# A two-layer decode step: the MLP's units in ten blocks of 128 and one of 96, in place of four padded stretches

## The chip, the cores and the metric

The kernel runs on one core of a Trainium2 chip. The metric is the device time of one execution in microseconds, as a median of several runs. All values are 32-bit floats.

## What is computed

One token `x` of 512 values goes twice through an attention block with a cached k and v, and a dense MLP. Both layers use the same weights and the same caches.

```python
def _A_ref(x, k_cache, v_cache, wq, wo):      # 32 heads, 4096 positions, 128 per head
    q = (x @ wq) by head
    scores = jnp.einsum("bhqd,bhkd->bhqk", q, k_cache) * (Dh ** -0.5)
    p = _softmax(scores, axis=-1)
    o = jnp.einsum("bhqk,bhkd->bhqd", p, v_cache)
    return o by token @ wo
def _B_ref(x, w1, b1, w2, b2):                # 512 -> 1376 -> 512
    h = _gelu(x @ w1 + b1)
    return h @ w2 + b2
x = x + _A_ref(_layernorm(x), k_cache, v_cache, wq, wo)
x = x + _B_ref(_layernorm(x), w1, b1, w2, b2)
x = x + _A_ref(_layernorm(x), k_cache, v_cache, wq, wo)
x = x + _B_ref(_layernorm(x), w1, b1, w2, b2)
```

The caches are 67 MB each and are read in both layers; w1 and w2 have 2.8 MB each.

## The kernel before, in words

The 32 heads are taken in eight groups of four. For each group, 8 MB of k and 8 MB of v come in loads over all 128 partitions into one large tile, `arena`, whose regions are used in turn. `scores` (L214) multiplies the query by k, `softmax` (L217 to L235) turns the scores into weights, `values` (L242) multiplies them by v, and `head_out` (L270, and L274 for the last group) multiplies by wo. Layer 0 goes through the groups upwards, layer 1 downwards, so that some of the caches stay in the arena from one layer to the next.

Every load goes through `load` (L84): the sync engine (SP) issues it to one hardware queue, in program order, when the region that it writes is free. The framework also lets SP hold a load until an earlier one has landed. TensorE's, VectorE's and SP's order near the MLP is written out by hand, by `pin`. `idle` (L374) is a matmul whose result nobody reads; some stand in the MLP between its steps.

`mlp` (L282) runs once in each layer. The 1376 hidden units are split into four stretches of 344, one for each quadrant `j` of 32 PSUM partitions, and the host pads each stretch of w2 and b1 with zeros to 352 = 11 x 32. `FB` = 11 counts the blocks of 32 units a quadrant, so a block is 128 units over all partitions. `HIDDEN` (L48) puts the blocks in three groups: 0 to 3, 4 to 7 and 8 to 10. `hidden(i)` (L290, matmuls at L296) computes one group with w1, 16 matmuls, each with the same number of columns: 128, 128 and 88. `turned` and `gelu` transpose the result and apply the activation, and L350 multiplies a block of 128 units by its 128 rows of w2, four matmuls a block (one for each quarter of the 512 outputs), adding up in `pM` over the eleven blocks. A 32-bit matmul stands as two instructions in the trace.

w1 is loaded once, in layer 0 (L476 and L487), and kept. w2 is loaded in each layer, in three parts over 128 partitions, `W2_PARTS` (L47): blocks 0 to 3, 4 to 7, 8 to 10 in layer 0, and 0 to 5, 6 to 8, 9 to 10 in layer 1. In layer 0 the last part takes the place of blocks 0 to 2, so it is issued in the middle of the MLP, behind block 3's matmuls (`follow`, L517 to L521, carried out at L352); behind it stand a piece of the next layer's k, and, behind the matmuls of blocks 5 and 7, two pieces of wq. In layer 1 the w2 parts are the last loads of the kernel (L477); behind them stands only the store of the output (L535).

Of the kernel before, what the change touches and what calls it, by code (L numbers as in the profile page):

```python
# [17 lines left out]
P = 128  # L18
D = 512
H, S, DH = 32, 4096, 128  # L20
F = 1376
G = 8
J = 4
C = 8
FJ = F // J
FB = 11
EPS = 1e-5
U = 512
KEPT = 6

NC = 4 * U
# [3 lines left out]
SPARE = 2 * BLOCK + STAY  # L35
# [4 lines left out]
AHEAD = 64  # L40
X_AT, B1_AT, B2_AT = 0, 8, 8 + FB
K2_HOME = 12 * NC

V1_HOME = *(2 * BLOCK + NC * c for c in range(5)), 8 * NC, 6 * NC, 7 * NC
W2_AT = tuple(SPARE + U * (c % 8) for c in range(FB)), tuple(2 * BLOCK + 2 * NC + U * c for c in range(FB))
PITCH = 1024
W2_PARTS = ((0, 4), (4, 8), (8, FB)), ((0, 6), (6, 9), (9, FB))  # L47
HIDDEN = ((0, 4), (4, 8), (8, FB))  # L48
W1_AT = (0, 4 * J * 32 * 4, 4 * J * 32 * 8)
# [10 lines left out]
def decode_layers(ctx: ExitStack, tc: tile.TileContext, k, v, w, w1, w2, out):  # L60
    nc = tc.nc
# [20 lines left out]
    arena = const.tile([P, ARENA], F32, name="arena")  # L82

    def load(at, src):  # L84
        t = arena[:, at : at + src.shape[-1]]
        tc.keep_in_program_order(nc.sync.dma_start(t, src))
        return t

    def pin(ins):
        tc.keep_in_program_order(ins)  # L90
# [34 lines left out]

    fixed = small("fixed", 2 * FB + 7)
    b1c, colsum, b2c = fixed[:, :FB], fixed[:, FB : 2 * FB], fixed[:, 2 * FB : 2 * FB + 4]
    negmean, one, power = (fixed[:, 2 * FB + 4 + i : 2 * FB + 5 + i] for i in range(3))
# [19 lines left out]
    pM, pN = pO[:, 2 * P : 3 * P], pO[:, 3 * P :]  # L148
# [7 lines left out]
    def of_32(t, n, i=0):  # L156
        return t[:, : 32 * n].rearrange("p (c q) -> p c q", q=32)[:, :, i]
# [15 lines left out]
    def mean_of(xs, s, at):  # L173
        nm = minus_mean(s, at)
        xc, sq, ss = small("xc", 4), small("sq", 4), small("ss")
        nc.vector.tensor_scalar(xc, xs[:, :, 0], nm, None, op0=ALU.add)
        nc.vector.scalar_tensor_tensor(sq, xc, 1.0, xc, op0=ALU.mult, op1=ALU.mult, accum_out=ss)
        return nm, ss, xc

    def rstd_of(ss, at):  # L180
        nv = minus_mean(ss, at)
        ve, r = small("ve"), small("rstd")
        tc.keep_in_program_order(
            nc.vector.tensor_scalar(ve, nv, -1.0, EPS, op0=ALU.mult, op1=ALU.add))
        nc.gpsimd.tensor_tensor(r, ve, power, op=ALU.pow)
# [96 lines left out]
    def mlp(xs, s, w1_t, w2_t, xb, rows, fill, follow):  # L282
        nm, ss, _ = mean_of(xs, s, pN[:, 0:1])
        nm_s, hs = small("nm_s"), pH[layer]
        if fill is None:
            nmr, cb, late = small("negm"), colsum, HIDDEN[0][1]
        nc.gpsimd.tensor_tensor(xb, xs[:, :, 0], b2c, op=ALU.add)
        nc.vector.tensor_copy(nm_s, nm)

        def hidden(i):  # L290
            at, first = hs[i], W1_AT[i]
            n = min(32 * HIDDEN[i][1], FJ) - 32 * HIDDEN[i][0]
            for c in range(4):
                for j in range(J):
                    f = first + n * (J * c + j)
                    pin(nc.tensor.matmul(at[32 * j : 32 * j + 2, :n], xs[:, c, :], w1_t[:, f : f + n],  # L296
                                         start=(c == 0), stop=(c == 3)))
                if i == 0 and c == VAR_AT:
                    rstd.append(rstd_of(ss, pN[:, 1:2]))
                    if fill is None:  # L300
                        nc.gpsimd.tensor_tensor(nmr, nm_s, rstd[0], op=ALU.mult)
                        nc.gpsimd.tensor_scalar(cb[:, late:], colsum[:, late:], nmr, None, op0=ALU.mult)
                        nc.gpsimd.tensor_tensor(cb[:, late:], cb[:, late:], b1c[:, late:], op=ALU.add)

        def turned(i):
            ht = work.tile([P, 32 * 4], F32, name="pt")
            n = HIDDEN[i][1] - HIDDEN[i][0]
            pin(nc.vector.transpose(ht[:, : 32 * n], hs[i][:, : 32 * n]))  # L308
            return ht

        def gelu(i, ht):
            b0, b1_ = HIDDEN[i]
            n = b1_ - b0
            h, u, g = (small("gelu_" + k, FB)[:, b0:b1_] for k in "hug")
            if fill is None and i > 0:
                pin(nc.vector.scalar_tensor_tensor(u, of_32(ht, n), rstd[0], cb[:, b0:b1_], op0=ALU.mult, op1=ALU.add))
            else:
                if i > 0:
                    nc.gpsimd.tensor_copy(colsum[:, b0:b1_], of_32(ht, n, 1))
                pin(nc.vector.scalar_tensor_tensor(h, of_32(ht, n, 1), nm_s, of_32(ht, n), op0=ALU.mult, op1=ALU.add))  # L320
                pin(nc.vector.scalar_tensor_tensor(u, h, rstd[0], b1c[:, b0:b1_], op0=ALU.mult, op1=ALU.add))
            nc.scalar.activation(g, u, AF.Gelu_apprx_tanh)
            if fill is not None and b1_ == FB:
                nc.scalar.activation(small("m"), g[:, :1], AF.Exp, scale=0.0)
            return g, turned(i + 1) if b1_ < FB else None

        rstd = []
        hidden(0)
        if fill is None:
            hidden(1)  # L330
            pin(nc.vector.transpose(rows[:, P : 2 * P], rows[:, :P]))
        ht = turned(0)
        if fill is not None:
            for _ in range(WARM):
                idle(fill, pO, 2 * P)
        hidden(1 if fill is not None else 2)
        if fill is not None:
            for _ in range(WARM):
                idle(fill, pO, 2 * P)
        for i, (b0, b1_) in enumerate(HIDDEN):  # L340
            if i == 1 and fill is not None:
                idle(fill, pS, 2 * P)
                hidden(2)
            g, ht = gelu(i, ht)
            if i == 1 and fill is not None:
                for _ in range(FILL):
                    idle(fill, pS, 2 * P)
            for c in range(b0, b1_):
                for j in range(J):
                    pin(nc.tensor.matmul(pM[32 * j : 32 * j + 1, :], g[:, c - b0 : c - b0 + 1],  # L350
                                         w2_t[c][:, P * j : P * (j + 1)], start=(c == 0), stop=(c == FB - 1)))
                for at, src in follow.get(c, ()):  # L352
                    load(at, src)
            if i == 1 and fill is not None:
                for _ in range(FILL - 1):
                    idle(fill, pS, 2 * P)
# [15 lines left out]
    w2_t = [[arena[:, at : at + U] for at in homes] for homes in W2_AT]  # L372
# [4 lines left out]
    for layer in range(2):  # L377
# [22 lines left out]
        for n, g in enumerate(order):  # L400
            first, final = n == 0, n == G - 1
# [65 lines left out]
            if layer == 1 and n == 0:  # L467
                wo_t = chunk(arena[:, PAIR : PAIR + NC])
            elif final:
                at = PAIR + NC * layer  # L470
                for a, b in WO_PARTS[layer]:
                    load(at + U * a, of_w(wo_at(g), 1)[:, U * a : U * b])
                wo_t = chunk(arena[:, at : at + NC])
                if layer == 0:
                    for i in range(2):
                        load(HELD + W1_AT[i], w1[:, W1_AT[i] : W1_AT[i + 1]])  # L476
                for a, b in W2_PARTS[layer][: 1 if layer == 0 else 3]:  # L477
                    load(W2_AT[layer][a], w2[:, U * a : U * b])
            else:
                t = load(PAIR, of_w(wo_at(g) if layer == 0 else wq_at(g - 1), 2))  # L480
                wo_t, wq_next = (chunk(t, i) for i in ((0, 1) if layer == 0 else (1, 0)))
            on = scaled_out_last(rl, pt, last_v, others) if final else scaled_out(rl, ot)
            if final:
                if layer == 0:
                    row_to_quadrants(row)
                    a, b = W2_PARTS[0][1]
                    load(HELD + W1_AT[2], w1[:, W1_AT[2] :])  # L487
                    load(W2_AT[0][a], w2[:, U * a : U * b])
                idle(last_v, pO, 256)
            head_out(on, wo_t, n)  # L490
            if final:
# [12 lines left out]
        at = work.tile([P, P], F32, name="pt")  # L504
# [7 lines left out]
            xb = of_32(ends, 4)  # L512
        follow = {}
        if layer == 0:
            a, b = W2_PARTS[0][2]
            first_k, next_wq = part(k, G - 2, 0, 1), of_w(wq_at(G - 2), 1)
            follow = {  # L517
                3: ((W2_AT[0][a], w2[:, U * a : U * b]), (SPARE + NC - U, first_k[:, NC - U :])),
                5: ((SPARE + NC, next_wq[:, : 2 * U]),),
                7: ((SPARE + NC + 2 * U, next_wq[:, 2 * U :]),),  # L520
            }  # L521
        mlp(x1, s1, w1_t, w2_t[layer], xb, *((None, last_v) if layer == 0 else (ends, None)), follow)
        if layer == 0:
# [4 lines left out]
            g = G - 2  # L528
# [9 lines left out]
def columns(a):  # L538

    return np.ascontiguousarray(a.reshape(J, 4, 32, -1).transpose(0, 2, 1, 3).reshape(P, 4, -1))  # L540
# [41 lines left out]
```

## Time and profile before

| | us |
|---|---|
| median of 3 runs | 677.32 (676.45 to 677.62) |
| the profiled execution | 677.48 |
| its span, first to last instruction | 675.6 |
| TensorE busy | 406.2 (60%) |
| VectorE busy | 115.1 (17%) |
| ScalarE busy | 27.3 (4%) |
| loads | 284.92 MB, 422 GB/s over the span |
| TensorE's mean granted clock | 0.798 |

The profiled execution is one run, and its span leaves out what lies ahead of the first instruction and behind the last. The trace names lines by the kernel's source, and a line can be that of a helper: all loads stand at L86. `in_w` stands for the three weight tensors alike. "DMA share" is the mean busy share of the sixteen DMA engines.

### The profile page before, as it was taken

What the parts mean: (1) busy time and instruction counts of PE and PEld (TensorE: products, weight loads), DVE (VectorE), ACT (ScalarE), POOL (GpSimd) and SP (SyncE); (2) the same over time, 40 slices, a digit from 0 to 9 for tenths busy, and PEclk for the clock granted to TensorE, in tenths of its full rate; (3) what the DMA queues carried; (4) which work ended last, traced back from release to release, by engine and by line L of the source; (5) the groups of instructions that cost most, each with busy time, mean ns of one, the idle gap of its engine ahead of it and who ended that gap; (6) DMA issues with size and microseconds to landing.
All of it is one profiled execution on the core that took longest, in us unless ns stands there. A gap on an engine that the chain in (4) does not pass through costs nothing.

```text
span 675.6 us, 6748 instructions
## 1 busy us (share of the span) xinstructions
PE 406.2 (60%) x3012; PEld 110.6 (16%) x3012; DVE 115.1 (17%) x369; ACT 27.3 (4%) x57; POOL 5.0 (1%) x24
## 2 busy tenths in 40 slices
PE   2644664465534854466798987574466544744797
PEld 1111111111111110111125321111111111110124
DVE  3002111121021201211022322120121011200212
ACT  0000000000000000001011200000000000000010
POOL 1000000000000000000000000000000000000000
PEclk9758767797678866877799998976797677975989
DMA  9999999999999999999999999999999999999996
GB/s 374 435 436 435 436 435 435 414 456 432 423 432 417 449 435 436 431 435 414 434 406 354 418 423 438 425 434 436 433 437 435 429 435 409 453 436 411 432 413 249
DMA packets 11268, 285.34 MB, mean 422 GB/s; under 512 B 1252, under 2 KB 1256, under 8 KB 3688
## 3 DMA queue, kind: packets, MB, share of 16 engines
q1 hardware_dynamic: 11240, 284.92, 98.6%
q8 instruction: 23, 0.38, 0.2%
q14 instruction: 5, 0.04, 0.0%
HBM read 284.92 MB, written 0.00 MB: 422 GB/s over the span
## 4 chain that ended last, share of the span: by engine, by line
PE 40%; DMA 39%; another core or an unknown queue 15%; DVE 4%; ACT 1%; issue 1%; ACTq 0%; SPq 0%; DVEq 0%
DMA arena<-in_v 34%; PE pO L242 20%; PE pS L214 12%; DMA arena<-in_w 4%; PE pB L270 4%; PE pO L208 1%; ACT arena L224 1%; PE pS L375 1%; PE pO L226 1%; DVE arena L246 1%; DVE smalls L218 1%; PE pO L375 0%; PE pO L350 0%; DVE arena L206 0%
## 5 line engine op out<-in xcount | busy, mean ns | idle before, releaser
L214 PE MATMUL pS<-arena,smalls 128*8 128x512 f32 x1024 | 145.9, 722 | 110.9 <-DMA arena<-in_k 110.1
L242 PE MATMUL pO<-arena,pt 128*4 128x512 f32 x1008 | 142.8, 714 | 84.3 <-DMA arena<-in_v 83.8
L214 PEld LDWEIGHTS pS<-arena,smalls 128*8 128x8 f32 x1024 | 30.0, 102 | 211.2 <-issue 190.5
L270 PE MATMUL pB<-arena,smalls 128*1 128x512 f32 x112 | 52.0, 608 | 20.0 <-DVE smalls L251 15.9
L242 PEld LDWEIGHTS pO<-arena,pt 128*4 128x4 f32 x1008 | 28.8, 97 | 186.5 <-issue 183.7
L218 DVE TENSOR_REDUCE smalls<-pS 128x1 f32<-128x512 f32 x16 | 11.1, 692 | 249.2 <-PE pS L214 249.2
L246 DVE STREAM_TRANSPOSE arena<-pO 128x512 f32<-128x512 f32 x16 | 11.5, 717 | 225.7 <-PE pO L242 225.7
L226 PE MATMUL pO<-ident,arena 128*128 128x128 f32 x64 | 13.2, 341 | 37.9 <-ACT arena L224 37.6
L224 ACT ACTIVATE arena<-pS,smalls 128x512 f32<-128x512 f32 x16 | 12.4, 777 | 535.7 <-DVE smalls L223 535.7
L206 DVE SCALAR_TENSOR_TENSOR arena<-arena,smalls 128x512 f32<-128x512 f32 x45 | 33.8, 752 | 1.6
L270 PEld LDWEIGHTS pB<-arena,smalls 128*1 128x1 f32 x112 | 8.5, 85 | 63.0 <-issue 35.2
L208 PE MATMUL pO<-smalls,arena 128*128 128x1 f32 x120 | 16.6, 260 | 3.3 <-DVE arena L206 3.3
L208 PEld LDWEIGHTS pO<-smalls,arena 128*128 128x128 f32 x120 | 15.3, 200 | 15.8 <-DVE arena L206 13.8
L226 PEld LDWEIGHTS pO<-ident,arena 128*128 128x128 f32 x64 | 8.5, 169 | 51.9 <-ACT arena L224 46.4
L375 PE MATMUL pO<-arena,ident 128*8 128x256 f32 (+1 forms) x42 | 14.4, 470 | 0.0
L375 PE MATMUL pS<-arena,ident 128*8 128x512 f32 (+1 forms) x34 | 14.0, 517 | 0.5 <-DVE pt L308 0.5
L204 DVE TENSOR_SCALAR arena<-arena,smalls 128x512 f32<-128x512 f32 x15 | 7.2, 481 | 2.7 <-DMA arena<-in_w 2.7
L209 DVE COPY smalls<-pO 128x4 f32<-128x4 f32 x15 | 2.5, 165 | 25.7 <-PE pO L208 25.7
L170 PE MATMUL pO<-smalls 128*32 128x1 f32 x64 | 2.0, 184 | 7.4 <-DVE smalls L164 6.4
L350 PE MATMUL pO<-arena,smalls 128*1 128x128 f32 x176 | 6.0, 272 | 0.7 <-DMA arena<-in_w 0.7
L230 DVE STREAM_TRANSPOSE smalls<-smalls 128x32 f32<-128x32 f32 x16 | 3.4, 212 | 17.4 <-ACT arena L224 17.4
L375 PEld LDWEIGHTS pO<-arena,ident 128*8 128x8 f32 x42 | 3.8, 90 | 7.9 <-issue 6.3
(92 smaller groups left out, 102.6 us busy)
## 6 DMA issues: line engine op xcount, KB each, us to landing
arena<-in_k SPq DMA_DIRECT2D x8, 4096.0 KB, 26.9
arena<-in_w SPq DMA_DIRECT2D x13, 2048.0 KB, 33.3
arena<-in_v SPq DMA_DIRECT2D x2, 4096.0 KB, 38.0
arena<-in_k SPq DMA_DIRECT2D x3, 2048.0 KB, 14.2
arena<-in_v SPq DMA_DIRECT2D x2, 2048.0 KB, 41.2
arena<-in_w SPq DMA_DIRECT2D x4, 1024.0 KB, 16.3
arena<-in_w SPq DMA_DIRECT2D x6, 512.0 KB, 12.1
arena<-in_v SPq DMA_DIRECT2D x2, 1024.0 KB, 42.9
```

Source lines behind the costliest of these rows:

```text
L204: pin(nc.vector.tensor_scalar(t, wt[:, 0, :], xc[:, 0:1], None, op0=ALU.mult))
L206: nc.vector.scalar_tensor_tensor(t, wt[:, c, :], xc[:, c : c + 1], t, op0=ALU.mult, op1=ALU.add)
L208: nc.tensor.matmul(at[:, j : j + 1], t[:, P * j : P * (j + 1)], one, start=True, stop=True)
L214: nc.tensor.matmul(pS[32 * j : 32 * j + C, :], z[:, j, C - 1 - c : 2 * C - 1 - c], kt[:, j, :], start=(c == 0), stop=(c == C - 1))
L218: nc.vector.tensor_reduce(mx[:, 0:1], pS, axis=AX.X, op=ALU.max)
L224: nc.scalar.activation(p, pS, AF.Exp, bias=bias[:, 0:1], scale=sc, accum_out=mx[:, 0:1])
L226: nc.tensor.transpose(pT[:, b].rearrange("p j r -> p (j r)"), p[:, P * b : P * (b + 1)], ident)
L242: nc.tensor.matmul(pO[32 * j : 32 * j + 4, :], pt[:, j, c, :], by_head(vt)[:, j], start=(i == 0), stop=(i == of - 1))
L246: nc.vector.transpose(ot[:, :512], pO)
L270: nc.tensor.matmul(pB[0:1, :], on[:, d : d + 1], wt[:, d, :], start=n == 0 and d == 0, stop=n == G - 2 and d == 3)
L350: pin(nc.tensor.matmul(pM[32 * j : 32 * j + 1, :], g[:, c - b0 : c - b0 + 1], w2_t[c][:, P * j : P * (j + 1)], start=(c == 0), stop=(c == ...
L375: pin(nc.tensor.matmul(at[:C, :n], ident[:, :C], t[:, 0, :n], start=True, stop=True))
```

## The change

The units are split without stretches: block `c` has units 128c to 128c + 127, and quadrant `j` has 32 of them; block 10 has only 96, so its fourth quadrant has none. w1 is laid out anew by the host with the same number of bytes, `hidden` gives each quadrant its own number of columns (in the third group 96, 96, 96 and 64), and w2 is padded at its end alone. `load_w2` loads the parts of w2. A part that holds block 10 comes as two loads: one over partitions 0 to 95 with all of its blocks, and one over partitions 96 to 127 with all but block 10. Block 10's matmuls read 96 rows. In layer 0 the last part is still issued behind block 3, ahead of the piece of k.

```diff
+FULL = F - P * (FB - 1)
...
+    def load_w2(layer, a, b):
+        at, whole = W2_AT[layer][a], min(b, FB - 1)
+        if b < FB:
+            load(at, w2[:, U * a : U * b])
+            return
+        pin(nc.sync.dma_start(arena[:FULL, at : at + U * (b - a)], w2[:FULL, U * a : U * b]))
+        if whole > a:
+            pin(nc.sync.dma_start(arena[FULL:, at : at + U * (whole - a)], w2[FULL:, U * a : U * whole]))
...
         def hidden(i):
             at, first = hs[i], W1_AT[i]
-            n = min(32 * HIDDEN[i][1], FJ) - 32 * HIDDEN[i][0]
+            b0, b1_ = HIDDEN[i]
+            ns = [32 * (b1_ - b0 - (b1_ == FB and j == J - 1)) for j in range(J)]
             for c in range(4):
-                for j in range(J):
-                    f = first + n * (J * c + j)
+                for j, n in enumerate(ns):
+                    f = first + sum(ns) * c + sum(ns[:j])
...
             for c in range(b0, b1_):
                 for j in range(J):
-                    pin(nc.tensor.matmul(pM[32 * j : 32 * j + 1, :], g[:, c - b0 : c - b0 + 1],
-                                         w2_t[c][:, P * j : P * (j + 1)], start=(c == 0), stop=(c == FB - 1)))
-                for at, src in follow.get(c, ()):
+                    rows_ = FULL if c == FB - 1 else P
+                    pin(nc.tensor.matmul(pM[32 * j : 32 * j + 1, :], g[:rows_, c - b0 : c - b0 + 1],
+                                         w2_t[c][:rows_, P * j : P * (j + 1)], start=(c == 0), stop=(c == FB - 1)))
+                for at, src in follow.get(c, ()) if c else ():
                     load(at, src)
+                if layer == 0 and c == 3:
+                    load_w2(0, *W2_PARTS[0][-1])
+                    for at, src in follow[0]:
+                        load(at, src)
...
                 for a, b in W2_PARTS[layer][: 1 if layer == 0 else 3]:
-                    load(W2_AT[layer][a], w2[:, U * a : U * b])
+                    load_w2(layer, a, b)
...
-            a, b = W2_PARTS[0][2]
             first_k, next_wq = part(k, G - 2, 0, 1), of_w(wq_at(G - 2), 1)
             follow = {
-                3: ((W2_AT[0][a], w2[:, U * a : U * b]), (SPARE + NC - U, first_k[:, NC - U :])),
+                0: ((SPARE + NC - U, first_k[:, NC - U :]),),
...
-    pad = 32 * FB - FJ
-    w2 = np.pad(a["w2"].reshape(J, FJ, D), ((0, 0), (0, pad), (0, 0)))
-    b1 = np.pad(a["b1"].reshape(J, FJ), ((0, 0), (0, pad)))
+    w2 = np.pad(a["w2"], ((0, P * FB - F), (0, 0))).reshape(FB, P, D)
+    b1 = np.pad(a["b1"], (0, P * FB - F)).reshape(FB, P)
...
```

## Rows read from the trace of the kernel before

**Rows 1.** The page: the span in 40 slices, and the hardware queue's packets, MB, share.

```profile
GB/s 374 435 436 435 436 435 435 414 456 432 423 432 417 449 435 436 431 435 414 434 406 354 418 423 438 425 434 436 433 437 435 429 435 409 453 436 411 432 413 249
...
q1 hardware_dynamic: 11240, 284.92, 98.6%
```

**Rows 2.** Busy time by stretch: length, engines (instructions), granted clock, DMA share, GB/s.

```profile
30.00:610.00 580.00, 346.26 (x2440) 91.91 (x2432) 97.41 (x305) 24.37 (x50) 1.78 (x6) 0.79 1.00 428
```

**Rows 3.** The chain of waits in the tail: start us, us, what.

```profile
627.56 32.33 DMA arena<-in_v
...
659.90 12.08 DMA arena<-in_w
...
672.02 0.66 PE pO L350 x16
...
672.71 0.29 DVE arena L534
```

**Rows 4.** The timeline in the tail, w2's matmuls: start, us, instructions, [idle before <-releaser].

```profile
668.95 1.49 PE L350 MATMUL pO<-arena,smalls 128*1 128x128 f32 x48
...
670.77 0.84 PE L350 MATMUL pO<-arena,smalls 128*1 128x128 f32 x24 [0.32 <-DMA arena<-in_w]
...
672.02 0.62 PE L350 MATMUL pO<-arena,smalls 128*1 128x128 f32 x16 [0.42 <-DMA arena<-in_w]
```

**Rows 5.** Busy time by stretch in the tail.

```profile
666.00:667.00 1.00, 0.79 (x33) 0.49 (x37) 0.49 (x6) 0.00 (x0) 0.20 (x1) 1.00 1.02 408
...
669.00:670.00 1.00, 1.00 (x47) 0.96 (x44) 0.73 (x3) 0.21 (x1) 0.08 (x1) 1.00 0.29 119
```

**Rows 6.** SP's own timeline at the turn, 364 to 371 us.

```profile
364.21 0.33 SPq L86 DMA_DIRECT2D arena<-in_w  x1
364.63 0.38 SPq L86 DMA_DIRECT2D arena<-in_k  x1
368.10 0.80 SPq L86 DMA_DIRECT2D arena<-in_w  x2
370.21 0.33 SPq L86 DMA_DIRECT2D arena<-in_k  x1
```

**Rows 7.** Loads issued from 352 to 380 us: count, size, us to landing.

```profile
arena<-in_w SPq DMA_DIRECT2D x2, 512.0 KB, 4.2
...
arena<-in_w SPq DMA_DIRECT2D x1, 768.0 KB, 5.0
...
arena<-in_k SPq DMA_DIRECT2D x1, 256.0 KB
```

**Rows 8.** The timeline at the turn: w1's matmuls, and w2's for the last blocks.

```profile
360.71 1.05 PE L296 MATMUL pS<-arena,smalls 128*2 128x128 f32 x32
...
364.83 0.79 PE L296 MATMUL pS<-arena,smalls 128*2 128x88 f32 x32
...
369.29 0.57 PEld L350 LDWEIGHTS pO<-arena,smalls 128*1 128x1 f32 x24 [0.47 <-issue]
369.32 0.83 PE L350 MATMUL pO<-arena,smalls 128*1 128x128 f32 x24
```

**Rows 9.** Busy time by stretch at the turn, quarters of a microsecond.

```profile
364.50:364.75 0.25, 0.25 (x2) 0.00 (x0) 0.00 (x0) 0.00 (x0) 0.00 (x0) 1.00 0.55 229
...
368.50:368.75 0.25, 0.25 (x3) 0.12 (x2) 0.00 (x0) 0.00 (x0) 0.00 (x0) 1.00 0.32 123
...
369.50:369.75 0.25, 0.25 (x16) 0.24 (x12) 0.00 (x0) 0.00 (x0) 0.00 (x0) 1.00 0.16 66
369.75:370.00 0.25, 0.25 (x17) 0.22 (x6) 0.00 (x0) 0.00 (x0) 0.00 (x0) 1.00 0.81 279
```

**Rows 10.** What SP waited for at the turn, 340 to 380 us: total, times, longest.

```profile
SPq L86 <- PE pO L350: 3.1, 3, 1.3
```

**Rows 11.** SP's own timeline at 628 us.

```profile
628.42 0.80 SPq L86 DMA_DIRECT2D arena<-in_v  x2
```

**Rows 12.** Loads issued from 620 us on: count, size, us to landing.

```profile
arena<-in_v SPq DMA_DIRECT2D x2, 512.0 KB, 33.6
```

More of the change, by code (lines that the diff above doesn't have):

```diff
@@ L487, in decode_layers @@
                     load(HELD + W1_AT[2], w1[:, W1_AT[2] :])
-                    load(W2_AT[0][a], w2[:, U * a : U * b])
+                    load_w2(0, a, b)
                 idle(last_v, pO, 256)
@@ L545 @@
         x=A_x, k=A_k_cache, v=A_v_cache, wq=A_wq, wo=A_wo, w1=B_w1, b1=B_b1, w2=B_w2, b2=B_b2).items()}
-    pad = 32 * FB - FJ
-    w2 = np.pad(a["w2"].reshape(J, FJ, D), ((0, 0), (0, pad), (0, 0)))
-    b1 = np.pad(a["b1"].reshape(J, FJ), ((0, 0), (0, pad)))
-    w1 = columns(a["w1"]).reshape(P, 4, J, FJ)
+    w2 = np.pad(a["w2"], ((0, P * FB - F), (0, 0))).reshape(FB, P, D)
+    b1 = np.pad(a["b1"], (0, P * FB - F)).reshape(FB, P)
+    w1 = columns(a["w1"])
     wq = columns(a["wq"]).reshape(P, 4, G, J, J, 32)
@@ L557 @@
         (X_AT, columns(a["x"])[:, :, 0]),
-        (B1_AT, b1.reshape(J, FB, 32).transpose(0, 2, 1).reshape(P, FB)),
+        (B1_AT, b1.T),
         (B2_AT, columns(a["b2"])[:, :, 0]),
@@ L565 @@
         w=w,
-        w1=np.concatenate([w1[..., 32 * a : 32 * b].reshape(P, -1) for a, b in HIDDEN], axis=1),
-        w2=w2.reshape(J, FB, 32, D).transpose(0, 2, 1, 3).reshape(P, FB * D),
+        w1=np.concatenate([w1[:, c, f : f + 32] for a, b in HIDDEN for c in range(4) for j in range(J)
+                           for f in range(P * a + 32 * j, min(P * b, F), P)], axis=1),
+        w2=w2.transpose(1, 0, 2).reshape(P, FB * D),
     )
```

## The prediction

> **What bounds the kernel now.** I first read the page by slices and by queue [rows 1]. In 37 of the first 39 slices the DMA engines moved 406 GB/s or more, and the loads of the one hardware queue took 98.6% of what sixteen engines could give in the span. So the kernel is a stream of 284.92 MB, and TensorE, 60% busy, is not the bound. Over the long middle the granted clock is 0.79 and the stream still moves 428 GB/s [rows 2]. In the units of the profile's size column (1024 bytes) that is 418 KB a microsecond. Two places remain where the change touches anything that may set the end: the turn between the layers, near 364 us, and the tail after 660 us.
>
> In the tail the chain of waits [rows 3] goes from a load of v to a load of w and from there straight to the last sixteen w2 instructions, the last addition and the store. The timeline [rows 4] shows the same from the engine's side: the 48 instructions of blocks 0 to 5 run without a wait, block 6 waits for a load until 670.77, and block 9 waits for the last part of w2 until 672.02. So this end is loads, to the last byte, although the queue is no longer full: by the stretches of one microsecond [rows 5], 408 GB/s moved in the 667th microsecond, 119 in the 670th. Some of the sixteen engines have finished and the slowest still works. Its pace is what counts: 1.25 us for the last 512 KB (670.77 to 672.02), or 410 KB/us, nearly the pace of the full stream.
>
> At the turn the last part of w2 (768 KB) is issued at 364.21 [rows 6] and lands 5.0 us later [rows 7], at 369.21. The matmuls that read it begin at 369.32, and what stood before their first weight load is named "issue", not a DMA [rows 8]. So the part lands about 0.1 us ahead of its use. After it the queue runs dry: 123 and then 66 GB/s at 368.5 and 369.5 [rows 9], because the next issue, at 368.10, stood behind a w2 matmul [rows 6, 10].
>
> **The change part by part.** The sum is made against the profiled execution: 677.48 us, a span of 675.6 and 1.88 around it, 0.16 above the median of 677.32.
>
> *Bytes.* w1 keeps its size: 16 pieces of 344 columns become, for the last blocks, three of 96 and one of 64 for each of four input rows, 352 in all as four of 88 were. w2 sheds 32 rows of its last block: 32 x 2 KB = 64 KB in each layer. The turn's load falls from 768 KB to 576 + 128 = 704, the tail's from 512 to 384 + 64 = 448.
>
> *Tail.* At the slowest engine's 410 KB/us, 64 KB are 0.16 us; at the stream's 418 they are 0.15. If rows spread over all engines as now, each engine has an eighth less of that part, and the landing moves from 672.02 to 671.87. No row shows a load over 96 or 32 partitions: all before cover 128 (the output's four rows aside). So the price is bounded: -0.15 us from below. From above, I take the row in which about half of the engines were at work: share 0.55 and 229 GB/s, 224 KB/us [rows 9]. Were both narrow loads held to that, 448 KB would take 2.0 us in place of 1.25, or +0.75. I take -0.15, because the nearest rows, those of the laggard tail, show each engine emptying its own share without waiting for the others.
>
> *Turn.* 64 KB less is 0.15 us of the queue again, but the queue runs dry there until TensorE releases the next issue, so a shorter load only lengthens the gap: I take 0. The bounds: -0.15, should the slowest engine be the one that never runs dry (369.21 plus 0.6 us for the 256 KB behind it [rows 7] is 369.8, just where the next load's data begin), and at half rate 704 / 224 = 3.1 us in place of 768 / 418 = 1.8, or +1.3, of which 0.1 is slack before the matmuls.
>
> *The added issues.* SP puts out two loads where it put out one; the distance from one issue to the next is 0.42 us (364.21 to 364.63) [rows 6]. At the turn the first 256 KB of k stand behind it and leave 0.42 later. Their matmuls are in the next layer, and SP then idles from 365.0 to 368.10, so the issues behind that are not moved. Without that cover it would be 0.42 us. In the tail SP has nothing behind it but the store at 673. But the added load takes a wait: SP holds each late load until the one eight issues before has landed, as the chain shows where the last part leaves at 659.90 with the landing of a v load issued at 627.56 [rows 3]. The added one waits for the next v load, issued at 628.42, with a median of 33.6 us to landing [rows 11, 12], thus until about 662.0. The load ahead of it lands at 670.77, so 8.8 us cover it: 0.
>
> *Matmuls.* The third group of hidden units is 96 wide where it was 88. Its instructions took 0.79 us at 88 columns and 1.05 at 128 [rows 8], so 6.5 ns a column, 0.05 us for eight more (the fourth quadrant, with 64, runs beside the others). In the tail it ends before the wait that ends at 670.77, so 0. At the turn it stands on TensorE's path, moves the issue at 368.10 to 368.15 and the later k loads as much. They find the loads before them still moving (two of 512 KB [rows 7], 2.4 us of the stream from about 369.75 [rows 9]), so I take 0, at most +0.05. Eight w2 instructions have 96 rows in place of 128: sixteen took 0.62 us [rows 4], so eight 0.31, and half of that either way would be 0.16 in each layer; no row has 96, the nearest have 128 and the same columns, and I take 0. VectorE and ScalarE do the same work on the same shapes.
>
> Sum: 677.48 - 0.15 = 677.33, and with the 0.16 between profiled run and median, 677.2.
>
> [...] The tail's rows show that late engines finish alone [rows 5], which is why I count the saving at all. [...]
>
> **The rivals.**
> *Serial.* The 96-row load takes as long as the whole part did, and the 32-row load follows at half the stream's rate. Tail: 64 KB at 224 KB/us, +0.29. Turn: 128 KB, +0.57, less 0.1 of slack, then TensorE is late by 0.47 and with it the k loads that wait for it. It decides from the point where the two together end later than 369.32. Sum +0.76: 678.1. For it: the even split of 128 rows over sixteen engines is gone. Against it: the slowest engine works alone at the end and meets nobody. [...]
> *Half.* Both narrow loads run on half of the engines. Tail +0.75, turn +1.2: 679.3, slower. For it: nothing but the missing row; against it: loads of 128 rows keep all sixteen at work [rows 1], and the length of a row stays what it was in the first of the two.
> *All bytes count.* The slowest engine never runs dry at the turn: -0.30, 677.0. For it: 369.8 against 369.75 above. Against it: what follows at 370.21 waits for matmuls.
> *Lag relieved.* The new split takes rows off just the engine that ends last. At most it saves the whole 1.25 us of the last part, and 0.15 at the turn: 675.9. For it: only the drain in [rows 5].
>
> **How the numbers follow.** Forecast 0.60, serial 0.18, all bytes count 0.11, half 0.07, lag relieved 0.04. About 0.2%, 1.35 us, is what a measurement can tell from no change. Forecast and all bytes count are within it, serial too (+0.8) with a small share beyond; half is beyond it (+2.0), the lag's relief just so (-1.4). So faster 0.04, same 0.86, slower 0.10. The range goes from all bytes count less the spread of the three runs (0.87 below their median), 676.2, to serial plus 0.6 of the same spread, 678.7; half and the lag's relief are left out.
>
> **What would show it.** The queue's bytes should fall by 0.13 MB. In the tail the last w2 matmuls should start about 1.1 us after block 6's wait ends, not 1.25; 1.5 says serial, 2.0 half. At the turn the last w2 matmuls should follow their filler matmuls with no DMA as releaser; a DMA wait of half a microsecond says serial, one of over a microsecond half. An issue of the k loads moved by more than 0.1 us with no such wait, or a stream below 428 GB/s in the middle, would mean that I have missed what the change touches.

## The result, and the profile after

The change makes the kernel slower: 680.5 us (679.85 to 681.48, six runs) against 677.62 (six runs beside it), a ratio of 1.0043 with a 95% interval of 1.0032 to 1.0054, so 2.9 us (2.2 to 3.7). The profiled execution took 680.87 us, with a span of 678.8, 3.2 us more than before. The forecast was 677.2, with a range up to 678.7.

The bytes are what the prediction said, 0.13 MB fewer on the page's queue line [rows 1]:

```profile
q1 hardware_dynamic: 11272, 284.79, 98.5%
```

The middle of the stream is not slower. From 30 to 360 us both kernels moved 429 GB/s, and from 380 to 610 both moved 433. What changed stands at the two places where w2's last part is loaded.

**The turn.** The timelines of SP and of TensorE after, against [rows 6] and [rows 8]:

```profile
364.22 0.34 SPq L95 DMA_DIRECT2D arena<-in_w  x1
364.61 0.42 SPq L97 DMA_DIRECT2D arena<-in_w  x1
365.12 0.37 SPq L87 DMA_DIRECT2D arena<-in_k  x1
368.63 0.82 SPq L87 DMA_DIRECT2D arena<-in_w  x2
372.15 0.33 SPq L87 DMA_DIRECT2D arena<-in_k  x1
```

```profile
364.90 0.84 PE L307 MATMUL pS<-arena,smalls 128*2 128x96 f32 x32
...
367.95 1.05 PE L362 MATMUL pO<-arena,smalls 128*1 128x128 f32 x32 [0.27 <-DMA arena<-in_w]
...
371.26 0.84 PE L362 MATMUL pO<-arena,smalls 128*1 128x128 f32 x24 [1.41 <-DMA arena<-in_w]
```

The two narrow loads leave when the one did. But TensorE now waits for a load before the last blocks, which it starts at 371.26 in place of 369.32, and the load of k behind them leaves at 372.15 in place of 370.21: 1.94 us later, and so do the next k loads. The matmuls of blocks 4 to 7 also wait a little, at 367.95. The loads' own rows say why (issued from 352 to 380 us: size, us to landing; the first line is of before, the others of after, against [rows 7]):

```profile
arena<-in_w SPq DMA_DIRECT2D x1, 1024.0 KB, 12.7
```

```profile
arena<-in_w SPq DMA_DIRECT2D x1, 1024.0 KB, 13.2
...
arena<-in_w SPq DMA_DIRECT2D x1, 576.0 KB, 6.5
...
arena<-in_w SPq DMA_DIRECT2D x1, 128.0 KB, 6.5
```

The 576 KB land 6.5 us after their issue, though the 768 KB took 5.0, and the 1 MB ahead of them, whole in both kernels, lands 0.5 us later too. That is no scatter: issued at 354.3 to 354.9 us in every trace, this load took 13.2 to 14.4 us in the five kernels with the narrow loads or the halves behind it (after, and below e2, e6, e8, e10), and 12.6 to 12.9 in the six others, e7 and e11 among them. The stretches of one microsecond show what the DMA engines did meanwhile (the last three columns are the granted clock, the DMA share and GB/s):

```profile
365.00:366.00 1.00, 0.74 (x32) 0.49 (x27) 0.12 (x1) 0.00 (x0) 0.10 (x1) 1.00 0.95 217
...
367.00:368.00 1.00, 0.73 (x8) 0.17 (x9) 0.00 (x0) 1.00 (x1) 0.00 (x0) 1.00 0.98 248
368.00:369.00 1.00, 1.00 (x33) 0.86 (x34) 0.00 (x0) 0.43 (x2) 0.00 (x0) 1.00 1.02 201
369.00:370.00 1.00, 0.85 (x6) 0.18 (x2) 0.00 (x0) 0.00 (x0) 0.00 (x0) 1.00 1.09 184
```

This is the line to learn to read: a share near 1 and 200 GB/s. A dry queue shows a low share at a low rate, as in [rows 9] (0.16 at 66); here the engines are busy all the time, 0.98 to 1.09, and move 184 to 248 GB/s, about half of the 429 of the long middle. One such microsecond alone proves little: before has 0.83 at 168 GB/s from 369 to 370, as loads begin, and after has 0.89 at 182 from 373 to 374, when the narrow loads have landed. From 367 to 370, three in a row with 0.98 or more at 184 to 248, are what before does not have; the loads by themselves below show it for 19 us on end.

**The tail.** The chain of waits and w2's matmuls after, against [rows 3] and [rows 4]:

```profile
629.12 34.28 DMA arena<-in_v
...
663.41 11.67 DMA arena<-in_w
...
675.22 0.66 PE pO L362 x16
```

```profile
672.07 1.49 PE L362 MATMUL pO<-arena,smalls 128*1 128x128 f32 x48 [0.65 <-DMA arena<-in_w]
...
674.11 0.84 PE L362 MATMUL pO<-arena,smalls 128*1 128x128 f32 x24 [0.55 <-DMA arena<-in_w]
675.22 0.62 PE L362 MATMUL pO<-arena,smalls 128*1 128x128 f32 x16 [0.27 <-DMA arena<-in_w]
```

The last matmuls start 1.11 us after block 6's, where it was 1.25: the sign that the prediction had named for itself is there. It proves nothing, because the whole loads ahead are late: blocks 0 to 5 waited for no load before and do now. The first narrow load leaves at 662.14, just as the last part did at 659.90 when the third v load had landed, and the last matmuls start 13.08 us later, where they started 12.12 later. These lines do not tell how much of that is lost in the tail itself; e2 and e3 below do. The windows again have a high share at half the rate:

```profile
669.00:670.00 1.00, 0.90 (x40) 0.77 (x40) 0.56 (x5) 0.00 (x0) 0.19 (x1) 1.00 0.91 207
```

### The profile page after: what moved, and what is told of

Read it like the earlier page. It is cut to its first block, busy times and chain, and to the rows that moved or that the text cites. A ratio compares the mean times of both kernels' runs of the same rounds, so it can differ in the third digit from the quotient of the medians.

```text
span 678.8 us, 6751 instructions
## 1 busy us (share of the span) xinstructions
PE 405.4 (60%) x3012; PEld 110.3 (16%) x3012; DVE 115.4 (17%) x369; ACT 27.3 (4%) x57; POOL 5.0 (1%) x24
## 4 chain that ended last, share of the span: by engine, by line
DMA 48%; PE 34%; another core or an unknown queue 13%; DVE 3%; issue 1%; ACT 1%; SPq 0%; ACTq 0%
DMA arena<-in_v 34%; PE pO L252 17%; PE pS L224 9%; DMA arena<-in_w 7%; DMA arena<-in_k 6%; PE pB L280 4%; PE pO L218 1%; PE pO L236 1%; PE pO L391 1%; ACT arena L234 1%; DVE arena L256 1%; DVE smalls L228 1%; PE pO L362 0%; DVE arena L216 0%
## 5 line engine op out<-in xcount | busy, mean ns | idle before, releaser
L252 PE MATMUL pO<-arena,pt 128*4 128x512 f32 x1008 | 138.1, 701 | 81.2 <-DMA arena<-in_v 80.8
L391 PE MATMUL pO<-arena,ident 128*8 128x256 f32 (+1 forms) x42 | 14.4, 470 | 0.0
L362 PE MATMUL pO<-arena,smalls 128*1 128x128 f32 (+1 forms) x176 | 6.0, 272 | 3.1 <-DMA arena<-in_w 3.1
L307 PE MATMUL pS<-arena,smalls 128*2 128x128 f32 (+2 forms) x160 | 5.0, 259 | 0.3 <-DMA arena<-in_w 0.2
## 6 DMA issues: line engine op xcount, KB each, us to landing
arena<-in_k SPq DMA_DIRECT2D x3, 2048.0 KB, 14.4
```

The source lines that it names most:

```text
L252: nc.tensor.matmul(pO[32 * j : 32 * j + 4, :], pt[:, j, c, :], by_head(vt)[:, j], start=(i == 0), stop=(i == of - 1))
L362: pin(nc.tensor.matmul(pM[32 * j : 32 * j + 1, :], g[:rows_, c - b0 : c - b0 + 1], w2_t[c][:rows_, P * j : P * (j + 1)], start=(c == 0), s ...
L391: pin(nc.tensor.matmul(at[:C, :n], ident[:, :C], t[:, 0, :n], start=True, stop=True))
```

## The experiments

The theory after the comparison: a load of fewer than 128 rows is slow for the rows that it writes, with the engines held meanwhile, as in the share of 0.98 to 1.09 above. The rivals: the new layout and its matmuls; the second load, with its issue and its wait; the number of rows as such; the rows that it reads.

### Undone, and at one place alone

```diff
 def load_w2(layer, a, b):
-    if b < FB:
+    if True:                       # e1: whole in both layers
...
+    if b < FB or layer == 1:       # e2: narrow in layer 0 alone
...
+    if b < FB or layer == 0:       # e3: narrow in layer 1 alone
```

e1: 

> The changed kernel with w2's last part loaded whole again, over 128 rows (768 and 512 KB), in both layers; the new layout of the units stays. If the narrow loads are the cause: the time of before, 677.6 (677.2 to 678.0), and the last w2 matmuls of layer 0 again near 369.3 without a wait for a load. If the layout, the 96-column matmuls or the 96-row matmuls are the cause: it stays near 680.5.

e2: 

> The changed kernel with the narrow loads in layer 0 alone; layer 1's last part is whole. If the turn passes its delay on to the end: about 1.9 to 2.2 us over before, so 679.5 to 679.8. If the stream makes up for the turn's delay in layer 1 and the tail is what costs: 677.6 to 678.0.

e3: 

> The changed kernel with the narrow loads in layer 1 alone; layer 0's last part is whole. If the two places add up: about 1.0 us over before, 678.6, and the loads of w2 ahead of the narrow ones land later than before by most of that. If the tail costs nothing: 677.5.

| | us | ratio to before, 95% |
|---|---|---|
| e1, whole in both | 677.0 | 0.9997 (0.9988 to 1.0006) |
| e2, narrow in layer 0 | 678.85 | 1.0023 (1.0015 to 1.0032) |
| e3, narrow in layer 1 | 678.29 | 1.0019 (1.0009 to 1.0029) |

With whole loads the changed layout takes the time of before, so neither the layout nor the matmuls of 96 columns and 96 rows cost anything that can be measured. The turn costs 1.6 us (1.0 to 2.2), the tail 1.3 (0.6 to 2.0), and the two make up the 2.9. In the median the turn's price is below the 1.9 that I expected, which its interval still holds: of the 1.94 us by which k loads were late near 380 us, the load of v near 415 kept 1.63 (415.94 against 414.31) and the load of k near 564 kept 1.40. Later issues do not tell: the load of v near 582 left 3.10 us later, the first one near 625 only 0.70.

e2 also shows how not to read the tail. Its loads there are all whole, and yet the last matmuls start 13.00 us after the last part was issued, as in after and not as before (chain of waits):

```profile
660.27 12.96 DMA arena<-in_w
673.27 0.66 PE pO L362 x16
```

What separates the two is how much was left to move. From 640 to 660 us and from 660 to 680, before moved 412 and 185 GB/s, 11.94 MB in all, e2 417 and 214, 12.62 MB, and after 418 and 218, 12.72 MB. By an estimate at 430 GB/s, near the 429 and 433 of the long stretches, e2's 0.68 MB more than before are 1.6 us, and it starts its last matmuls 1.25 later; after's 0.78 MB are 1.8 us, and it starts them 3.20 later. So in after some 1.4 us are lost past 640 us, which agrees with the tail's 1.3.

In e3's trace the whole loads ahead of the narrow ones are the late ones. The loads issued from 620 us on, first e1 and then e3:

```profile
arena<-in_w SPq DMA_DIRECT2D x1, 1536.0 KB, 16.3
...
arena<-in_w SPq DMA_DIRECT2D x1, 768.0 KB, 13.2
```

```profile
arena<-in_w SPq DMA_DIRECT2D x1, 1536.0 KB, 18.2
...
arena<-in_w SPq DMA_DIRECT2D x1, 768.0 KB, 15.2
```

Both of e3's are 2 us later than e1's, though they are whole in both. (e3's profiled execution is longer than its median, so the 2 us are that run's.) Over all traces the 768 KB took 14.5 to 16.2 us in the five with the narrow loads or the halves behind them in the tail, 13.2 to 13.6 in five others and 14.2 in e2, where the stream alone was late. Why these loads are late is not shown.

### A second load, but of whole rows

```diff
-        pin(nc.sync.dma_start(arena[:FULL, at : at + U * (b - a)], w2[:FULL, U * a : U * b]))
-        if whole > a:
-            pin(nc.sync.dma_start(arena[FULL:, at : at + U * (whole - a)], w2[FULL:, U * a : U * whole]))
+        load(at, w2[:, U * a : U * whole])
+        load(at + U * (whole - a), w2[:, U * whole : U * b])
```

> The last part in two loads as in the change, but cut by blocks and not by rows: all blocks but the last over 128 rows, then block 10 over 128 rows; bytes as before. If a second load, its issue and its wait are the cost: near 680.5. If it is the number of rows: 677.6 (677.2 to 678.0).

676.75 us, 0.9994 (0.9985 to 1.0002). The second issue and its wait are covered, as the prediction had it.

### Loads by themselves

Eight loads in a row from SP into eight places, and a small write by VectorE to each place when it has landed; the next stage waits for all. Nothing else of the reference is computed, and each of these kernels (e5, e9, e12) ran once.

```python
for i, (a, b) in enumerate(stage):
    nc.sync.dma_start(places[i][a:b, :], k[s % G][a:b, N * i : N * (i + 1)])
for i in range(8):
    nc.vector.memset(places[i][:, :8], 0.0)
```

> Loads of k alone, nothing else of the reference: twelve stages of eight loads, each row 8 KB; a stage starts when the one before has landed. Rows by stage: 128; 0-95; 96-127; 0-95 and 96-127 in turn; 0-63; 64-127; 0-63 and 64-127 in turn; 0-111; 0-31; 128 and 0-95 in turn; 128 and 96-127 in turn; 128. Whole loads move about 430 GB/s: 8.4 MB in 19.5 us plus some 2 us of start. If a narrow load only has fewer bytes: 0-95 takes 14.6, 96-127 4.9, 0-63 9.8 plus the start. If it runs on half of the engines: double these (29, 9.8, 19.5), with a DMA share near 0.5. If all engines work but get in each other's way at the rows' side: a share near 1 at about half the rate, 0-95 in 19.5 or more, and the stages that mix narrow and whole loads slower than the sum of their parts at their own rates.

VectorE's writes give the landings (start, us, instruction, idle before). Two each from the stages of 0-95, 96-127 and 128 rows, all of 8 KB a row:

```profile
41.97 0.07 DVE L45 MEMSET place<- 128x8 f32 x1 [3.03 <-DMA place<-in_k]
45.05 0.07 DVE L45 MEMSET place<- 128x8 f32 x1 [3.01 <-DMA place<-in_k]
...
62.24 0.07 DVE L45 MEMSET place<- 128x8 f32 x1 [1.23 <-DMA place<-in_k]
63.52 0.07 DVE L45 MEMSET place<- 128x8 f32 x1 [1.22 <-DMA place<-in_k]
...
251.13 0.07 DVE L45 MEMSET place<- 128x8 f32 x1 [2.43 <-DMA place<-in_k]
253.62 0.07 DVE L45 MEMSET place<- 128x8 f32 x1 [2.43 <-DMA place<-in_k]
```

Read the distance from one start to the next: 2.49 us a load of 128 rows, 3.08 of 96, 1.28 of 32. The load of 96 rows takes longer than the one of 128, with a quarter less in it. By stages (length, VectorE, GpSimd, clock, DMA share, GB/s; in this order 0-95, 96-127, 128 rows):

```profile
34.00:53.00 19.00, 0.39 (x6) 0.00 (x0) 1.00 1.01 254
59.00:67.00 8.00, 0.39 (x6) 0.00 (x0) 1.00 0.84 166
248.00:262.00 14.00, 0.39 (x6) 0.00 (x0) 1.00 1.01 425
```

The share of 0-95 is 1.01: the engines are all held, so it isn't half of them at work. (The 0.84 of 96-127 takes in the stage's start; from 60 to 65 us it is 1.02, at 203 GB/s.) The change's own pair, 0-95 and 96-127 in turn, took 4.3 us, nearly the sum of its two. The other stages: 64 rows, 0-63 or 64-127, 2.5 to 2.6 us a load, and 4.7 to 4.8 for the pair; 0-111 2.9; 0-31 1.3. In turn with whole loads, 96 rows cost their 3.1 (5.6 the pair). In turn with whole loads, 96-127 cost about 1.7 (4.2 the pair, single pairs from 3.5 to 5.2) in place of 1.28: on average the pair takes longer than the sum of its two, 3.8.

### The number of rows, or which rows

In each of these the two loads of `load_w2` are replaced (`put` stands for the load of the same part of `w2` into the same part of `arena`):

```diff
-        put(rows :FULL, blocks a to b)
-        put(rows FULL:, blocks a to whole)
+        put(rows :FULL, blocks a to b); put(rows FULL:, blocks a to b)          # e6
+        put(all rows, blocks a to whole); put(rows :FULL, blocks whole to b)    # e7
+        put(rows :64, blocks a to b); put(rows 64:, blocks a to b)              # e8
+        put(rows FULL:, blocks a to whole); put(rows :FULL, blocks a to b)      # e10
+        put(rows 0:P:2, blocks a to b); put(rows 1:P:2, blocks a to b)          # e11
```

e6: 

> The changed kernel with the last part in the same two row ranges (0-95, 96-127), but with all blocks in both: 768 and 512 KB as before. If narrow loads cost for their rows and not for what is left out: 680.5 or somewhat more. If the unequal lengths of the two are the cost: 677.5.

e7: 

> All blocks but the last over 128 rows, and only block 10's 512 columns over rows 0-95: the same bytes saved as in the change, with one narrow load of 192 KB in each layer in place of 704 and 448 KB. If the cost goes with the bytes in narrow loads: 192 of 704 KB at the turn and 192 of 448 in the tail, 0.27 x 1.6 + 0.43 x 1.3 = 1.0 over before, 678.4. If it is a cost of each narrow load: 2.9 over two pairs, so about 1.4, 678.8. If saved bytes count: 677.0.

e8: 

> The last part in two loads of 64 rows, all blocks, 768 and 512 KB. If any load of fewer than 128 rows makes the engines collide: 680 to 682. If it is 96 rows that do not divide as 128 do, and 64 do: 677.5.

e10: 

> The change with the two narrow loads in the other order: rows 96-127 first, then 0-95. If what costs is the time that each takes in the queue: 680.5, as the change. If it is the last one to land, alone, that counts, and the order of a short and a long one matters: 679.5 or 681.5.

e11: 

> The last part in two loads of 64 rows with all blocks, as the halves, but cut into even and odd rows in place of 0-63 and 64-127; same bytes, same number of loads. If the number of rows in a load, or its being one of two, is the cost: 681.2 as the halves, 4.2 over before. If it is which rows one load writes: within 0.6 of before, 677.0 (676.4 to 677.6).

| | us | ratio to before, 95% |
|---|---|---|
| e6, 0-95 and 96-127, all blocks | 681.45 | 1.0063 (1.0051 to 1.0075) |
| e7, only block 10 narrow | 677.14 | 0.9995 (0.9986 to 1.0003) |
| e8, 0-63 and 64-127, all blocks | 681.24 | 1.0062 (1.0049 to 1.0076) |
| e10, 96-127 first | 680.48 | 1.0055 (1.0041 to 1.0069) |
| e11, even and odd rows, all blocks | 677.68 | 1.0002 (0.9993 to 1.0011) |

e8 and e11 are the pair that decides: both load the last part in two loads of 64 rows, with the same bytes. One costs 4.2 us, the other nothing that can be measured. In e11 the last matmuls of the turn wait for no load:

```profile
369.34 0.92 PE L361 MATMUL pO<-arena,smalls 128*1 128x128 f32 x22
```

e6 shows that what is left out was never the cost: with no byte saved, the same two ranges cost 4.3 us. e7 missed both prices that I had put on it, 678.4 and 678.8. By e5's rates an estimate is +0.15 at either place (2.02 us for 1.87 at the turn, 1.39 for 1.25 in the tail), 0.3 in all, where its interval ends at +0.2; the 0.1 us of slack at the turn is the size of the difference, but no run shows that it is the reason. Its bytes saved don't show either. The order of the two (e10) makes no difference to the change that can be measured.

### Which rows, read or written

The stages of e5 with other rows, and, in e12, with other rows read than written:

```diff
-        nc.sync.dma_start(places[i][a:b, :], k[s % G][a:b, N * i : N * (i + 1)])
+        nc.sync.dma_start(places[i][which, :n], k[s % G][source, N * i : N * i + n])
```

> Loads of k alone again, nothing else of the reference. Seven stages of eight loads: 128 rows of 6 KB (as many bytes as 96 of 8 KB); then rows of 8 KB: 0-63; 32-95; every second row (64); every fourth (32); 16-111; 32-127. If the row count or the bytes of a load set the pace: 32-95 and every second row take the 2.5 us a load of 0-63, every fourth 1.3, 16-111 and 32-127 the 3.1 of 0-95. [...] Then six stages in the order and the sizes of the tail of layer 1: three loads of 1 MB and one of 768 KB whole, and behind them 512 KB whole; rows 0-95 and 96-127 as in the change; the two in the other order; block 10 alone narrow; and the first two again. By e5's price of a load alone (3.08 us for 96 rows of 8 KB, 1.28 for 32): the change's order ends 0.6 us later than the whole one, block 10 alone narrow 0.15 later. If narrow loads also hold up whole loads ahead of them: over 1 us later.

> Loads of k alone, nothing else of the reference; rows of 8 KB, eight loads a stage. 128 rows; then 64 rows, written to 0-63 from 0-63, to 0-63 from even rows, to 0-63 from 32-95, to even rows from 0-63, to 32-95 from 0-63; 128 and 0-63 in turn; 128 and 32-95 in turn; then the tail's order three times whole and three times narrow in turn. If the rows written set the pace: the three loads to 0-63 take 2.5 us each whatever they read, and the two others 1.25 though they read 0-63. If the rows read do: the reverse. The narrow tail ends 0.6 us after the whole one by e5's prices; if it holds up whole loads ahead of it, more than 1.

In e9, 64 rows of 32-95 take half the time of 64 rows of 0-63. The landings of 32-95:

```profile
57.90 0.07 DVE L50 MEMSET place<- 128x8 f32 x1 [1.61 <-DMA place<-in_k]
59.15 0.07 DVE L50 MEMSET place<- 128x8 f32 x1 [1.18 <-DMA place<-in_k]
60.40 0.07 DVE L50 MEMSET place<- 128x8 f32 x1 [1.19 <-DMA place<-in_k]
```

1.25 us a load in the steady part against 2.55, and 1.24 for every second row. (Both stages began unevenly, so their means are 1.47 and 1.40. Every fourth row, 32 in all, never became steady: 0.63 to 1.72 us, mean 0.97, more than half of the 1.24 of every second row.) 128 rows with a 6 KB row, as many bytes as 96 with 8 KB, took 1.9 us in the whole load of the tail's order, not 3.08. 16-111 took 3.0, and 32-127 2.9.

e12 crosses what is read with what is written. Two landings of rows 0-63 written from even rows, then two of rows 32-95 written from 0-63:

```profile
61.11 0.07 DVE L49 MEMSET place<- 128x8 f32 x1 [2.46 <-DMA place<-in_k]
63.65 0.07 DVE L49 MEMSET place<- 128x8 f32 x1 [2.47 <-DMA place<-in_k]
...
121.82 0.07 DVE L49 MEMSET place<- 128x8 f32 x1 [1.20 <-DMA place<-in_k]
123.04 0.07 DVE L49 MEMSET place<- 128x8 f32 x1 [1.16 <-DMA place<-in_k]
```

2.54 us apart for rows 0-63, though what they read is spread over all rows, and 1.22 for rows 32-95, though they read 0-63. The two other crossings say the same: 0-63 written from 32-95 took 2.53, even rows written from 0-63 took 1.24. So it is the rows written in the chip's memory, not the rows read.

The tail's order by itself, from the first issue to the last landing, in both runs: whole 12.7, 12.8, 13.3, 13.4 and 12.8 us, narrow 13.9, 13.4, 13.3, 13.2 and 13.3. The means are about 0.45 us apart, near the 0.6 by e5's rates and below the 1.3 that the kernel pays, but the single values overlap. Once each, the turned order took 13.3 and block 10 alone narrow 13.9, far more than the 0.15 over whole that I expected; a scatter of this size says little. The replay has neither the v and wo loads ahead nor the long stream before them.

## Why the prediction was wrong

**The step that failed** is the price of the narrow loads: "I take -0.15, because the nearest rows, those of the laggard tail, show each engine emptying its own share without waiting for the others", and at the turn "I take 0". Those rows were all of loads over 128 rows, which move 425 GB/s at a share of 1.01 (e5). Over rows 0-95 the engines are held just as much and move 254. So fewer bytes took longer: in place of -0.15 and 0 stand +1.3 (0.6 to 2.0) and +1.6 (1.0 to 2.2).

**The rivals.** Serial had the 32 rows: half the rate is what e5 measured (1.28 us for a quarter of the bytes that take 2.49). But no run shows 96 rows taking as long as 128, the term that its sum rests on: they took a quarter longer, 3.08 for 2.49. Why they do is open: no run here shows how the engines share out 96 rows. Shown is that the engines are held (1.01 at 254 GB/s, e5) and that the rows written decide (e8 and e11, e9, e12). Half came nearest to the price (+2.0 of the 2.9), for a reason that the DMA share of 1.01 rules out. Serial's chance of 0.18 and half's of 0.07 were too low for a load that no row showed.

**The bounds** were +0.75 for the tail and +1.3 for the turn, from rows at half rate. By an estimate from e5's rates, the narrow loads alone cost +0.6 in the tail (1.86 us for 1.25) and +1.1 at the turn (2.95 for 1.87), 1.7 together. The bounds held those, and not the 2.9. What they left out is that narrow loads also delay the whole loads ahead of them, by 0.5 us or more at the turn (13.2 to 14.4 for 12.6 to 12.9) and in the tail too, by an amount that the traces do not settle. How much of the other 1.2 us that makes is not shown, and stays open: the replay of the tail alone did not give it back.

**The other steps.** The bytes fell as said. The 96-column group took 0.84 for 0.79 us, the 0.05 forecast, and the second issue and its wait were covered (e4). At the turn the lateness passed through TensorE to the k loads, the way that serial described: 1.94 us there, 1.6 of them left at the end by e2's median. That saved bytes count for 0.15 us in the tail is left open: no run resolves it.

Place told more than number: 0-63 ran at half the rate (2.55 us for 512 KB), 0-31 no faster per byte (1.3 for 256 KB), and the two halves nearly one after the other (4.7 to 4.8 us for the pair), but 32-95, and every second row, moved 512 KB in 1.25 us, 419 GB/s, near the 425 of 128 rows.

## What to carry to other kernels

Look at which partitions a load writes before you count its bytes: cut to 96 rows, a load of 128 took a quarter longer (3.08 us for 2.49, e5). Pad to 128 rows, as before did, or, for 64, take rows like 32-95 or every second one (1.25 us in e9, where 0-63 took 2.55), and keep what is narrow small (e7, 677.14 us). None of the three choices of 96 rows tried here was fast (2.9 to 3.1 us). When a trace has no row for a form that the change introduces, measure it first, or give the case that it is slow the weight of the unknown; and look for its cost in the loads ahead of it too.

## What the runs showed of the hardware

Sixty-four rows took 2.55 us (0-63) or 1.25 (32-95) for the same 512 KB, by their place alone (e9). A load of 96 rows, in each of three places (0-95, 16-111, 32-127), took 2.9 to 3.1 us for 768 KB, longer than the 2.49 of 1 MB over 128 rows (e5, e9). At the turn a whole load of 1 MB took 13.2 to 14.4 us in the kernels with the narrow loads or the halves behind it in the queue, and 12.6 to 12.9 in the others. The DMA share reads 1.01 both at 425 GB/s (128 rows) and at 254 (0-95, both e5), so it does not tell a full stream from a slow one; only the rate beside it does.
